# Sinkhorn block attention with a mixture of experts, one core: routing weights spread by GpSimd from a single row, batch 0's second queries laid side by side and transposed whole

## The chip, the cores and the metric

The kernel runs on one core of a Trainium2 chip. The metric is the device time of one launch in microseconds (us). A core has TensorE (PE in the profile, its weight loads PEld), VectorE (DVE), ScalarE (ACT), GpSimd (POOL) and SyncE (SP), which run side by side, each in the order of its own instructions, and wait for one another on semaphores. TensorE writes into PSUM; VectorE and ScalarE carry results from there to SBUF. DMAs are issued by an engine's queue (here SP's and POOL's) and carried out by 16 shared DMA engines.

## The reference

Two parts, the second on the output of the first. Shapes: 4 batches, 8 heads, 768 tokens, head size 64; 8 blocks of 96 tokens; 4 experts with 512 inputs, 1024 hidden units, 512 outputs.

```python
for _ in range(5):                       # P = sort_net, [4, 8, 8, 8]
    P = np.exp(P - P.max(-1, keepdims=True))
    P = P / (P.sum(-1, keepdims=True) + 1e-9)
    P = P / (P.sum(-2, keepdims=True) + 1e-9)
k_sorted = einsum('bhij,bhjcd->bhicd', P, k_blocks)     # v likewise
scores = q_blocks @ k_sorted.T / sqrt(64)               # within each block
attn = softmax(scores) @ v_sorted
x = attn.transpose(0, 2, 1, 3).reshape(3072, 512)
p = domain_probs / (domain_probs.sum(-1, keepdims=True) + 1e-9)
out = sum(p[:, e:e+1] * (np.maximum(x @ w1[e], 0) @ w2[e]) for e in range(4))
```

## The kernel before

**Batch 0 first, then chunks.** The Sinkhorn rounds (L310 to L330, ScalarE's exponentials and VectorE's sums on 32 partitions) stand at the start. Meanwhile TensorE runs matmuls on a constant tile (`warm`, L276) and transposes the first half of batch 0's queries. Batch 0's attention is written out by hand (from L1390 on) in quarters, so that expert 0's first layer (`group0`, L704) can begin before the attention is done. From then on the experts work in 12 chunks of 256 tokens, `(b, c)` with three chunks a batch: `chunk_first` (L815) computes a group of hidden units into one of two PSUM tiles (`psM`, two buffers), and VectorE's L821 applies the ReLU and the routing weight and writes the tile `Hb`; the second layer (L799, L860, in the last chunks L1296) uses a scheme of block sums made by VectorE (L770 to L791). Attention stages of the following batch are put between these by a plan of slots (`PLANS`): `st_q` transposes queries by DMA (L413), `st_v` and `st_k` mix the values and keys (L391, L425), `st_s` and `st_a` compute scores and outputs (L444, L479). In the last chunks POOL multiplies by the routing weight (L1166).

**The routing weights.** L821 multiplies hidden units (on partitions) by a weight that depends on the token (along the row), so every partition needs the same row of weights. VectorE normalises `domain_probs` (`spread_weights`, L246 to L252) and SP writes the result to a scratch tensor `p_dram` in DRAM, in two parts (L256, the first batch; L258, the rest). `load_p` (L230) then reads `p_dram` back with a broadcast over 128 partitions, into a tile `pb` of 4 experts x 256 tokens in f32, of which there is one buffer. Chunk (0, 0) loads all four experts' rows; expert 1's row of chunk (0, 1) is loaded by `load_p_one` (L241) into the place of the first queries (`Tt[3]`), and experts 2 and 3 of that chunk by L230 within `chunk(0, 0)`. Expert 0 of batch 0 doesn't use `pb`.

**Batch 0's queries.** They are loaded into `q0` (in `Tt[3]`) in two halves (L152), with heads of group 0 on partitions 0 to 63 and of group 1 on 64 to 127. `h_q` (L288) transposes 64x64 pieces, 24 a group, into PSUM and a copy brings them to `qT0`. The first half goes by `h_q` with ScalarE's copies (L292), the second by `h_q_both` (two groups, one PSUM tile, then a copy on VectorE and one on ScalarE, L301) as the first of the steps in `later`, which `next_stages` puts between the matmuls of expert 0's second layer (`second_layer0`, L741).

**POOL's queue.** All loads of k, v, q and the weights are POOL's (`load_natural` L113, `load_queries` L126, `load_w1` L139, `load_w2` L146, L1456 and L1475 for parts). There are eight semaphores for them, so that each waits for the landing of the one eight before it. Between them stand POOL's own steps, in the order of the program: masks at the start, `builds(1)` (four multiplies, L364 and L372, which prepare batch 1's mixing matrices), and in `chunk(0, 0)` additions to the output (L953 to L995). `homes`, `sums0` and `sums2` steer where hidden units lie and when weight sums are made; the change doesn't touch them.

**The order around the change.** On ScalarE, batch 0's stretch from 20 us on reads: `h_x(1, act, [0])` (a copy of attention outputs, L628), two evacuations of `group0` (L717), `h_k(0, 1, act)` (mixed keys, L532), two more evacuations, the query copy L301. On POOL: the load of w2 of expert 1, of w2 of expert 2, of w1 of expert 3, of half of w2 of expert 3, `builds(1)`, then batch 1's first loads.

Of the kernel before, what the change touches and what calls it, by code (L numbers as in the profile page):

```python
# [2 lines left out]

# [15 lines left out]
def kernel(  # L19
# [20 lines left out]
    P = 128  # L40
# [182 lines left out]

    pbs = {}

    def load_p(b, c, es=range(E), pb=None):
        if pb is None:
            pb = moe.tile([P, E, 2 * P], F32, name=f"pb_{b}_{c}", tag="pb", bufs=1)
        n = len(es)
        nc.sync.dma_start(  # L230
            pb[:, ds(es[0], n)],
            p_dram[ds(es[0], n), ds(b * S + 2 * c * P, 2 * P)].rearrange("(o e) x -> o e x", o=1).broadcast_to(
                [P, n, 2 * P]
            ),
        )
        return pb

    def load_p_one(b, c, e):

        pb = Tt[3].rearrange("p a f x -> p (a f x)")[:, 0:4 * P].bitcast(F32)  # L240
        nc.sync.dma_start(pb, p_dram[ds(e, 1), ds(b * S + 2 * c * P, 2 * P)].broadcast_to([P, 2 * P]))  # L241
        return pb

    def spread_weights():

        nc.vector.tensor_reduce(p_den, p_in, AX.X, ALU.add)  # L246
        yield
        nc.vector.tensor_scalar(out=p_den, in0=p_den, scalar1=1e-9, scalar2=None, op0=ALU.add)
        yield
        nc.vector.reciprocal(p_den, p_den)  # L250
        yield
        nc.vector.tensor_tensor(  # L252
            p_out.rearrange("p e t -> p t e"), p_in, p_den.broadcast_to([P, NT, E]), ALU.mult
        )
        p_rows = p_dram.rearrange("e (p t) -> p e t", t=NT)
        nc.sync.dma_start(p_rows[0:S_P], p_out[0:S_P])  # L256
        pbs[(0, 0)] = load_p(0, 0)
        nc.sync.dma_start(p_rows[S_P:P], p_out[S_P:P])  # L258
        yield

# [11 lines left out]
    def warm(n):  # L272
        ps = psM.tile([P, 4, P], F32, tag="ps", name=f"ps_w_{state['n']}")
        state["n"] += 1
        for m in range(n):
            nc.tensor.matmul(ps[:, m % 4, :], dummy, dummy, start=True, stop=True)  # L276
# [3 lines left out]
    def h_q(qd, hf, copy, ps=None):  # L280

        if ps is None:
            ps = psa([P, 2, R, 64], F16, f"ps_q_{qd}_{hf}")
        rows = ds(64 * qd, 64)
        for sg in range(2):
            for r in range(R):
                for hh in range(2):
                    nc.tensor.transpose(  # L288
                        ps[ds(D * hh, D), sg, r, :], q0[rows, hf, 2 * sg + hh, r, :], ident[rows, rows]
                    )  # L290
        if copy:
            copy(qT0[qd][:, :, hf], ps[:])  # L292

    def h_q_both(hf, copy):

        ps = psa([P, 2, 1024], F16, f"ps_q_{hf}")
        pss = [ps[:, qd, 0:2 * R * 64].rearrange("p (s r x) -> p s r x", s=2, r=R) for qd in range(2)]
        for qd in range(2):
            h_q(qd, hf, None, pss[qd])
        for qd in range(2):  # L300
            copy[qd](qT0[qd][:, :, hf], pss[qd])  # L301


    srow = const.tile([GH, NB, 1], F32, name="srow")
    scol = const.tile([GH, NB, 1], F32, name="scol")
    sn16 = const.tile([GH, NB, NB, CP], F16, name="sn16")
    warm(84)
    p_steps = spread_weights()
    for it in range(5):
        nc.scalar.activation(sn[:], sn[:], AF.Exp, bias=0.0, scale=1.0)  # L310
# [226 lines left out]
    def h_k(qd, hf, copy, pool=psa):  # L537
        mixed("k", qd, mix_half("k", qd, hf, pool), 0, HB, copy)
# [295 lines left out]
    def chunk(b, c, slot, done=()):  # L834
# [120 lines left out]
        def f2():  # L955
            tt(oa1, product("p2", blk(1, 0), "b21"), oa1, ALU.add)
            slot()
# [522 lines left out]
    builds(1)  # L1480

    later = [
        [(h_q_both, 1, (vec, act)), (h_w, 1, vec)],
        [(h_s, 0, 2), (h_s, 1, 2)],
        [(h_w, 0, vec)],
        [(h_a, 0, 2)],
# [10 lines left out]
                f(*args)  # L1497

    second_layer0(0, next_stages)
    load_queries(1, range(2))  # L1500
    load_natural(1, "v", 0, 2, lambda: load_w2_part(3, DH))
    load_natural(1, "k", 0, 2)
    load_natural(1, "v", 1)
    load_natural(1, "k", 1)
    chunk_first(0, 0, [1, 2], 1, next_stages)
    pb_1 = load_p_one(0, 1, 1)
    h_sums(1, 4)
    for w in range(1, 5):
        h_sums(2, w)
# [41 lines left out]
_INS = ['q', 'k', 'v', 'sort_net', 'moe_domain_probs', 'moe_w1', 'moe_w2']  # L1551
_OUTS = [((3072, 512), 'float32')]
# [25 lines left out]
```

## Time and profile before

| What | Before |
|---|---|
| median of 3 runs | 358.61 us (358.37 to 359.99) |
| the profiled execution | 358.21 us |
| its span | 356.3 us |
| DMA traffic | 40.26 MB, mean 113 GB/s |
| HBM | 41.88 MB read, 6.34 MB written |
| `pb<-p_dram` of 512 KB (4 of them) | 5.8 us from issue to landing, median |
| `pb<-p_dram` of 384 KB (3) | 7.1 us |
| `T<-p_dram` of 128 KB (1) | 12.6 us |
| w loads of 1024 KB (4) | 27.2 us |

The span is the time from the first to the last record of the profiled execution; the rest of its 358.21 us lies around it. Busy times of engines overlap. An instruction's row gives its start, its length, its engine and line, the tile written and the ones read, with their shape; in brackets stands how long its engine had been idle before it and what ended that. A DMA's time from issue to landing holds its waiting behind other transfers.

### The profile page before, as it was taken

Reading aid. Unit: us, or ns where it says so; the run is one execution under the profiler, and the core shown is the slowest. Engines: PE = TensorE matmul, PEld = TensorE weight load, DVE = VectorE, ACT = ScalarE, POOL = GpSimd, SP = SyncE. Lnnn points to the kernel's source line nnn. Section 1 sums busy time; section 2 is a strip of 40 time slices with the busy share of each in tenths; the row PEclk is TensorE's granted clock in tenths of the full one; section 3 lists DMA queues with packets and bytes.
Section 4 is the critical chain, followed back from the end, with each engine's and each line's share of the span. In section 5 each row is a group of like instructions: output and inputs, shape, how many; then the busy total and the mean of one; then the engine's idle time right before and its main releaser. Section 6 shows DMA issues by size and latency. Waiting matters only on the chain.

```text
span 356.3 us, 9511 instructions
## 1 busy us (share of the span) xinstructions
PE 350.4 (98%) x3948; PEld 305.5 (86%) x3948; DVE 277.5 (78%) x555; ACT 170.1 (48%) x302; POOL 137.6 (39%) x154
## 2 busy tenths in 40 slices
PE   8899999999999999999999999999999999999996
PEld 8686857888888888988899888888888888888886
DVE  5766787779798687778879988896678886588963
ACT  2653330452425445368847259830288611598301
POOL 8766112466022420000626318840068800188400
PEclk9999999999999999999999999999999999999999
DMA  8999999999999999743995410005200014100021
GB/s 104 203 205 230 212 209 194 207 195 167 195 180 166 195 116 203 138 88 44 180 205 91 107 74 0 2 1 136 78 26 3 2 37 141 62 0 2 0 75 46
DMA packets 74762, 40.26 MB, mean 113 GB/s; under 512 B 41568, under 2 KB 70496, under 8 KB 74720
## 3 DMA queue, kind: packets, MB, share of 16 engines
q0 software_dynamic: 38720, 19.93, 43.2%
q1 hardware_dynamic: 35856, 19.67, 27.2%
q8 instruction: 31, 0.51, 0.6%
q14 instruction: 11, 0.09, 0.1%
q10 hardware_dynamic: 144, 0.07, 0.1%
HBM read 41.88 MB, written 6.34 MB: 135 GB/s over the span
## 4 chain that ended last, share of the span: by engine, by line
PE 95%; DVE 3%; issue 0%; DMA 0%; ACT 0%; DVEq 0%
PE ps_h L815 18%; PE ps_Q L1296 18%; PE ps_p L799 12%; PE ps_X L1153 10%; PE ps_Z L1153 7%; PE ps_Q L1153 7%; PE ps_Z L1296 6%; PE ps_h L704 3%; PE ps_o L741 3%; PE ps_p L860 3%; PE ps_a L479 2%; PE ps_s L444 2%; PE ps_k L425 1%; PE ps_v L391 1%; PE ps_mv L521 1%; PE ps_a L593 0%
## 5 line engine op out<-in xcount | busy, mean ns | idle before, releaser
L815 PE MATMUL ps_h<-xT,w 128*128 128x256 f16 x576 | 67.5, 273 | 0.0
L815 PEld LDWEIGHTS <-w 128*128 128x128 f16 x576 | 55.2, 98 | 7.3
L821 DVE SCALAR_TENSOR_TENSOR Hb<-ps_h,pb 128x1024 f16<-128x1024 f32 x34 | 41.5, 1223 | 17.8 <-PE ps_h L815 17.6
L1153 PEld LDWEIGHTS <-w 128*128 128x128 f16 x480 | 43.6, 98 | 4.7
L1166 POOL TENSOR_TENSOR arena<-tmp,pb 128x512 f16<-128x512 f32 x12 | 15.2, 1276 | 65.7 <-PE ps_Z L1153 49.8
L1296 PEld LDWEIGHTS <-Hb 128*128 128x128 f16 x320 | 31.1, 98 | 3.5
L1165 ACT ACTIVATE tmp<-tmp 128x512 f32<-128x512 f32 x46 | 29.0, 632 | 3.9 <-DVE tmp L1203 3.9
L1296 PEld LDWEIGHTS <-Sb 128*128 128x128 f16 x304 | 28.2, 98 | 3.0
L1153 PEld LDWEIGHTS <-arena 128*128 128x128 f16 x312 | 27.7, 98 | 2.8
L451 ACT ACTIVATE ET<-ps_s 96x768 f16<-96x768 f32 x24 | 18.1, 802 | 25.2 <-PE ps_s L444 25.0
L434 ACT CAST kT<-ps_k 64x384 f16<-64x384 f32 x48 | 22.7, 473 | 13.3 <-PE ps_k L425 12.3
L126 POOL DMA_DIRECT2D arena<-in_q_dram x24 | 19.9, 842 | 20.8 <-DMA q_ring<-arena 17.7
L1153 PE MATMUL ps_X<-ET,arena 128*128 128x256 f16 x168 | 25.2, 272 | 0.0
L1296 PE MATMUL ps_Q<-w,Hb 128*128 128x256 f16 x192 | 24.6, 273 | 0.0
L799 PEld LDWEIGHTS <-Hb 128*128 128x128 f16 x232 | 21.9, 98 | 3.0
L1159 DVE SCALAR_TENSOR_TENSOR Hb<-ps_X,pb 128x512 f16<-128x512 f32 x27 | 18.7, 692 | 7.0 <-PE ps_X L1153 7.0
L1173 ACT COPY ps_X<-ps_Z 128x512 f32<-128x512 f32 x27 | 15.4, 571 | 17.8 <-PE ps_Z L1153 17.8
L1153 PE MATMUL ps_Z<-xT,w 128*128 128x256 f16 (+1 forms) x176 | 22.5, 258 | 0.0
L785 DVE TENSOR_TENSOR Sb<-Hb 128x512 f16<-128x512 f16 x33 | 20.6, 646 | 0.0
L1180 ACT COPY tmp<-ps_X 128x512 f32<-128x512 f32 x26 | 15.2, 586 | 9.2 <-PE ps_X L1153 6.6
L1159 DVE SCALAR_TENSOR_TENSOR Hb<-ps_Z,pb 128x512 f16<-128x512 f32 x27 | 18.4, 683 | 1.3 <-PE ps_Z L1153 1.3
L1203 DVE TENSOR_TENSOR tmp<-ps_Q,tmp 128x512 f32<-128x512 f32 x26 | 17.7, 683 | 0.8 <-PE ps_Q L1153 0.8
(270 smaller groups left out, 744.3 us busy)
## 6 DMA issues: line engine op xcount, KB each, us to landing
w<-in_moe_w_dram POOLq DMA_DIRECT2D x4, 1024.0 KB, 27.2
w<-in_moe_w_dram POOLq DMA_DIRECT2D x6, 512.0 KB, 19.7
arena<-in_k_dram POOLq DMA_DIRECT2D x7, 384.0 KB, 7.6
arena<-in_v_dram POOLq DMA_DIRECT2D x7, 384.0 KB, 8.1
vs<-arena SPq DMA_DIRECT2D x36, 66.0 KB, 5.3
arena<-in_q_dram POOLq DMA_DIRECT2D x24, 96.0 KB, 7.5
out_dram<-ob SPq DMA_DIRECT2D x9, 256.0 KB, 2.0
pb<-p_dram SPq DMA_DIRECT2D x4, 512.0 KB, 5.8
```

The source lines that it names most:

```text
L126: nc.gpsimd.dma_start(t[:, h // 2, :, h % 2, :], q[b, h].rearrange("(t p) d -> p t d", p=P))
L434: nc.scalar.copy(kT[ds(D * hh, D), r], pk[ds(D * r, D), hh].rearrange("p a (i c) -> p a i c", c=CP),)
L451: nc.scalar.activation(ETs[2 * (pr % 2) + hh][:, 0:S].rearrange("c (a x) -> c a x", a=2), pss[hh][0:BLK, :, 0:HS], AF.Exp, bias=0.0, scale ...
L785: tt(sm[0], blk(0, 1), blk(1, 1), ALU.add)
L799: nc.tensor.matmul(ps, lhs(e, f), Ts[e][rhs][:, f, :], start=(first and e == es[0] and f == 0), stop=(done and e == es[-1] and f == KH - 1 ...
L815: nc.tensor.matmul(ps[:, f, :], w1sb[e][:, kc, ds((4 * g + f) * P, P)], xT[:, kc, ds(2 * c * P, 2 * P)], start=(kc == 0), stop=(kc == NKC ...
L821: nc.vector.scalar_tensor_tensor(out=Hb[:, homes.get(e, e), ds(4 * g, 4), :], in0=ps[:], scalar=0.0, op0=ALU.max, in1=weights(e).broadcast ...
L1153: nc.tensor.matmul(dst[:, ds(f * cols, cols)], a[lhs][:, k, ds((f0 + f) * P, P)], t[rhs][:, k, :], start=(first and f == 0 and k == 0), st ...
L1159: nc.vector.scalar_tensor_tensor(out=home(i, j), in0=src.rearrange("p (f x) -> p f x", f=m), scalar=0.0, op0=ALU.max, in1=weight(j).broadc ...
L1165: nc.scalar.activation(src, src, AF.Relu, bias=0.0, scale=1.0)
L1203: tt(t12, Q, u2, ALU.add)
L1296: nc.tensor.matmul(ps, lhs(e, f), Ts[e][rhs][:, f, part], start=(first and e == 0 and f == 0), stop=(e == E - 1 and f == KH - 1), skip_gro ...
```

## The change

- `load_p_one` and chunk (0, 0)'s and (0, 1)'s share of `load_p` are replaced: SP reads the rows of `p_dram` into partition 0 of the tile alone (`load_rows`), and POOL copies partition 0 to all 128 (`spread`, an instruction `partition_broadcast` from a GpSimd library that is loaded for it, after the load of w2 of expert 1). Chunk (0, 0) reads experts 1 to 3 only. The first `spread` stands between the loads of w2 of experts 1 and 2, the one for (0, 1)'s expert 1 ahead of batch 1's first query loads, the last in `chunk(0, 0)`. POOL's multiplies after the load run from the new library, which has them too; the library that was there first is loaded again at the end. Chunks from (0, 2) on are as before.
- The second half of batch 0's queries: ScalarE copies it from `q0` into `q1` (in `Tt[1]`), with two groups' heads beside each other in a row of 128 (`pair_q`, 128x1536 f16), and `half_q` transposes 12 pieces of 128x128 instead of 48 of 64x64. The two copies out of PSUM stay, with another stride.
- `h_x(1, ..., [0])` copies on VectorE instead of ScalarE.
- The first warm-up block has 69 matmuls instead of 84.

```diff
+    def pb_tile(b, c):
+        return moe.tile([P, E, 2 * P], F32, name=f"pb_{b}_{c}", tag="pb", bufs=1)
...
     def load_p_one(b, c, e):
         pb = Tt[3].rearrange("p a f x -> p (a f x)")[:, 0:4 * P].bitcast(F32)
-        nc.sync.dma_start(pb, p_dram[ds(e, 1), ds(b * S + 2 * c * P, 2 * P)].broadcast_to([P, 2 * P]))
+        pb = pb.rearrange("p (o x) -> p o x", o=1)
+        load_rows(pb, b, c, [e])
+        spread(pb)
         return pb
+
+    def load_rows(dst, b, c, es):
+        nc.sync.dma_start(
+            dst[0:1], p_dram[ds(es[0], len(es)), ds(b * S + 2 * c * P, 2 * P)].rearrange("(o e) x -> o e x", o=1)
+        )
+
+    def spread(dst):
+        nc.gpsimd.partition_broadcast(dst, dst[0:1])
...
-        pbs[(0, 0)] = load_p(0, 0)
+        pbs[(0, 0)] = pb_tile(0, 0)
+        load_rows(pbs[(0, 0)][:, 1:E], 0, 0, range(1, E))
...
+    q1 = Tt[1].rearrange("p a f x -> p (a f x)")[:, 0:2 * R * P].rearrange("p (s r x) -> p s r x", s=2, r=R)
+
+    def pair_q():
+        nc.scalar.copy(
+            q1.rearrange("p s r (h d) -> p s h r d", h=2),
+            q0[:, 1].rearrange("p (s h) r d -> p s h r d", h=2),
+        )
+
+    def half_q(copies):
+        ps = psa([P, 2, 1024], F16, "ps_q1")
+        for sg in range(2):
+            for r in range(R):
+                nc.tensor.transpose(ps[:, sg, ds(r * P, P)], q1[:, sg, r], ident[:])
         for qd in range(2):
-            h_q(qd, hf, None, pss[qd])
-        for qd in range(2):
-            copy[qd](qT0[qd][:, :, hf], pss[qd])
+            copies[qd](
+                qT0[qd][:, :, 1],
+                ps[:, :, 0:R * P].rearrange("p s (r q x) -> p s r q x", r=R, q=2)[:, :, :, qd],
+            )
...
-    warm(84)
+    warm(69)
...
-        pbs[nxt] = load_p(*nxt, range(first, first + 1))
-        rest = lambda: load_p(*nxt, range(first + 1, E), pbs[nxt])
         late = b == c == 1
-        if not late:
-            rest()
+        if nxt == (0, 1):
+            pbs[nxt] = pb_tile(*nxt)
+            load_rows(pbs[nxt][:, 2:E], *nxt, range(2, E))
+        else:
+            pbs[nxt] = load_p(*nxt, range(first, first + 1))
+            rest = lambda: load_p(*nxt, range(first + 1, E), pbs[nxt])
+            if not late:
+                rest()
...
         f2()
+        spread(pbs[nxt][:, 2:E])
         next(steps)
...
-    h_x(1, act, [0], ps_s01)
+    h_x(1, vec, [0], ps_s01)
     evacuate00()
...
     h_k(0, 1, act)
+    pair_q()
     group0(1, 1, 0, [0, 1])
...
     load_w2(1)
+    nc.gpsimd.load_library(library_config.all_libraries[10])
+    spread(pbs[(0, 0)][:, 1:E])
     load_w2(2)
...
-        [(h_q_both, 1, (vec, act)), (h_w, 1, vec)],
+        [(half_q, (vec, act)), (h_w, 1, vec)],
...
     second_layer0(0, next_stages)
+    pb_1 = load_p_one(0, 1, 1)
     load_queries(1, range(2))
...
     chunk_first(0, 0, [1, 2], 1, next_stages)
-    pb_1 = load_p_one(0, 1, 1)
...
-    chunk_first(0, 1, [1], 1, next_stages, lambda e: pb_1.rearrange("p (o x) -> p o x", o=1))
+    chunk_first(0, 1, [1], 1, next_stages, lambda e: pb_1)
...
         last_second(g + 1, upper=True)
+    nc.gpsimd.load_library(library_config.standard)
```

More of the change, by code (lines that the diff above doesn't have):

```diff
@@ L5 @@
 import concourse.tile as tile
-from concourse import mybir
+from concourse import library_config, mybir
 from concourse.bass import ds
@@ L224 @@
     pbs = {}
+    def pb_tile(b, c):
+        return moe.tile([P, E, 2 * P], F32, name=f"pb_{b}_{c}", tag="pb", bufs=1)
     def load_p(b, c, es=range(E), pb=None):
         if pb is None:
-            pb = moe.tile([P, E, 2 * P], F32, name=f"pb_{b}_{c}", tag="pb", bufs=1)
+            pb = pb_tile(b, c)
         n = len(es)
@@ L292, in h_q @@
             copy(qT0[qd][:, :, hf], ps[:])
-    def h_q_both(hf, copy):
-        ps = psa([P, 2, 1024], F16, f"ps_q_{hf}")
-        pss = [ps[:, qd, 0:2 * R * 64].rearrange("p (s r x) -> p s r x", s=2, r=R) for qd in range(2)]
+    q1 = Tt[1].rearrange("p a f x -> p (a f x)")[:, 0:2 * R * P].rearrange("p (s r x) -> p s r x", s=2, r=R)
[9 more added lines that the diff above has]
+                nc.tensor.transpose(ps[:, sg, ds(r * P, P)], q1[:, sg, r], ident[:])
         for qd in range(2):
-            h_q(qd, hf, None, pss[qd])
-        for qd in range(2):
-            copy[qd](qT0[qd][:, :, hf], pss[qd])
+            copies[qd](
+                qT0[qd][:, :, 1],
+                ps[:, :, 0:R * P].rearrange("p s (r q x) -> p s r q x", r=R, q=2)[:, :, :, qd],
+            )
     srow = const.tile([GH, NB, 1], F32, name="srow")
```

## The prediction

> **What bounds the kernel now.** I read the page's busy shares first, then the chain of waits, then the timeline of the stretches the change touches (the start to 12 us, 18 to 48 us, 62 to 76 us), and last the DMA issues there. The busy shares and the chain:
>
> ```profile
> PE 350.4 (98%) x3948; PEld 305.5 (86%) x3948; DVE 277.5 (78%) x555; ACT 170.1 (48%) x302; POOL 137.6 (39%) x154
> ...
> PE 95%; DVE 3%; issue 0%; DMA 0%; ACT 0%; DVEq 0%
> ```
>
> The chain that ended last is TensorE work for 95% of 356.3 us. The 3% of VectorE is nearly all before 11.60 us, in the five Sinkhorn rounds; no DMA stands in it. So TensorE work taken out of the chain is worth its length, a DMA or POOL step brought forward is worth nothing, and one made late costs as soon as TensorE runs out of other work.
>
> **The fewer warm-up matmuls** (84 to 69). Timeline of the start (start, length, engine, line; idle before in brackets):
>
> ```profile
> 1.06 6.74 PE L276 MATMUL ps_w<-Hb 128*128 128x128 f16 x84 [1.06 <-DVE Hb L157]
> ...
> 8.51 1.85 PE L276 MATMUL ps_w<-Hb 128*128 128x128 f16 x30
> 11.60 0.26 PE L342 MATMUL ps_R<-ident,sn 32*128 32x32 f16 x4 [1.24 <-DVE sn L330]
> ```
>
> Late warm-up matmuls take 1.85/30 = 62 ns, so 15 fewer end TensorE's lead-in 15 x 62 = 0.9 us sooner. The next step, L342, waits for VectorE's L330 whatever TensorE does, so the 0.9 us turns into idle time: 1.24 becomes about 2.1 us. The first query transposes between the two blocks need DMAs issued at 1.28 and 2.0 us that took 4.1 and 4.2 us: there by 6.2, before the 6.9 us at which they would now start. Cost 0; if the idle time slows what follows, rival D.
>
> **Forty-eight small transposes become twelve full ones.** From the chain of waits, first the ones removed, then the nearest full-width ones:
>
> ```profile
> 28.79 0.78 PE ps_q L288 x45
> 29.57 0.58 PE ps_w L548 x8
> ```
>
> L288 takes 0.78 us of the chain. Twelve full ones cost 12 x 62 = 0.74 us by the warm-up row, 12 x 0.58/8 = 0.87 us by L548's: between -0.04 and +0.09 us. I take 0: fewer instructions, not less time. The two copies out of PSUM (L301: VectorE 0.56, ScalarE 0.80 us) keep their 128x768 elements and their order: 0.
>
> **The ScalarE copy that lays the queries side by side** (`pair_q`) is new, 128x1536 f16, queued behind L532's second key copy:
>
> ```profile
> 23.81 0.82 ACT L532 CAST kT<-ps_mk 128x768 f16<-128x768 f32 x1
> 26.32 0.81 ACT L717 ACTIVATE Hb<-ps_h 128x768 f16<-128x768 f32 x1 [1.69 <-PE ps_h L704]
> ```
>
> L532 takes 0.48 us for 384 elements and 0.82 for 768, so 0.34 per 384 more and 0.82 + 2 x 0.34 = 1.50 us for 1536 (two copies of 768 as L292's would be 1.6). It runs 24.63 to 26.13 or 26.23, within the 1.69 us of idle time. Behind it waits L717, whose PSUM tile L741 at 27.76 needs; L717 ended at 27.13, so there are 0.6 us more. Moving `h_x(1, ..., [0])` from ScalarE (0.48 at 22.05) to VectorE (0.56 by its twin at 24.39) starts ScalarE up to 0.4 us sooner; VectorE had nothing from 21.93 to 23.02. Its input, the second query halves, was issued at 12.40 and 13.0 us and took 10.0 and 10.2: there at 23.2, before 24.2. Cost 0; without that cover, each us of `pair_q` beyond 0.8 us of slack is a us on TensorE.
>
> **The weights of the experts: rows and a POOL broadcast for a broadcasting DMA.** Removed before 40 us: one DMA of 512 KB (three quarters of it needed) and one of 128 KB, and later 384 KB; each is now a DMA of 1 to 3 KB into one partition, and a `partition_broadcast` on POOL. A library load comes ahead of the first, and POOL runs in order, so everything behind it slides: three weight loads, four builds, then the loads of batch 1. POOL before (its timeline), then the reader of the tile and what VectorE does behind it (VectorE's timeline):
>
> ```profile
> 21.71 1.76 POOL L146 DMA_DIRECT2D w<-in_moe_w_dram  x2 [0.38 <-DMA w<-in_moe_w_dram]
> 23.50 0.75 POOL L139 DMA_DIRECT2D w<-in_moe_w_dram  x1
> 26.10 0.89 POOL L1475 DMA_DIRECT2D w<-in_moe_w_dram  x1 [1.86 <-DMA w<-in_moe_w_dram]
> ```
>
> ```profile
> 38.79 1.23 DVE L821 SCALAR_TENSOR_TENSOR Hb<-ps_h,pb 128x1024 f16<-128x1024 f32 x1 [1.63 <-PE ps_h L815]
> 39.93 0.19 DVE L606 RECIPROCAL rz<-ps_a 96x8 f32<-96x8 f32 x1
> 40.15 0.69 DVE L607 TENSOR_TENSOR xsl<-ps_a,rz 96x512 f16<-96x512 f32 x1
> 40.78 1.23 DVE L821 SCALAR_TENSOR_TENSOR Hb<-ps_h,pb 128x1024 f16<-128x1024 f32 x1
> 41.92 0.19 DVE L606 RECIPROCAL rz<-ps_a 96x8 f32<-96x8 f32 x1
> 42.15 0.69 DVE L607 TENSOR_TENSOR xsl<-ps_a,rz 96x512 f16<-96x512 f32 x1
> ```
>
> The deadline is 38.79: from there VectorE runs without a gap until 42.84, and TensorE's L624 starts at 42.91 on its result. Load and broadcast together may take 38.79 - 22.55 (the load of w2 of expert 1 is out by then) = 16.2 us; each us beyond is one on TensorE.
>
> *The load.* No row shows one. From below: the only table load in the trace, ScalarE's at 0.74 us, 1.28 us. From above: a load whose code comes through busy DMA engines as late as the slowest transfer issued in this stretch, 33.3 us (L1475's). Nearest are the small transfers on the other queue at the same time: 5.5 us (12 KB), 12.2 (36 KB), 12.6 (128 KB). I take 10 us.
>
> [...]
>
> *The broadcast.* Also without a row: POOL's 128x128 copy took 0.30 us (L194 0.29), so 768 elements are 0.30 if size hardly counts and 6 x 0.30 = 1.8 us in proportion; from above, the DMA that did the same, 10.4 us. I take 1.8. Its rows are asked for at 25.51, once the p_dram write of 5.5 us is in, and are there by 31.0 (5.5, as the 12 KB took) or 35.9 at worst (10.4). So the broadcast ends at 32.6 + 1.8 = 34.4, or 37.7 with the latest rows: 4.4 or 1.1 us ahead of the deadline. Cost 0, with ends of 0 and (22.55 + 33.3 + 10.4 - 38.79) = +27 us.
>
> *What slides behind it.* From 34.4 the three weight loads are issued (0.8 each), the builds run (4 x 1.05), then a broadcast of 256 (0.6): 41.7, and batch 1's first query load goes out there instead of at 31.02. The transfers are behind a queue that stays full: issued at 21.71, w2 of expert 1 took 25.1 us and landed at 46.8; the next two megabytes, issued at 22.6 and 23.5, landed at 51.9 and 56.8, each after what stood ahead of it. So nothing is lost if the next is issued before about 43, and POOL, whose L113 at 47.35 waited for that same landing at 46.8, has caught up there. Against it: 640 KB fewer to move at 1 MB per 4.9 us (51.9 to 56.8) brings later landings 3 us forward, but who waited for them is one TensorE row, L391 at 65.38, with 0.19 us. Gain 0 to 0.2.
>
> *The second chunk's weights.* L230's pair, issued at 63.82, took 8.6 and 7.0 us; L821 reads them at 75.10. Rows in 5.5 us and a broadcast of 512 (1.2 by the same proportion) make 70.5. Behind that broadcast POOL's two query loads go out at 70.5 and 71.3 instead of 65.25 and 66.1. They took 10.8 and 10.7 us, because k's 384 KB, issued at 60.76 with 13.7 us, had to land first, at 74.5; out at 71.3 they are still in time for that place, or, where the queue is 3 us further, land 4.8 us after issue (the shortest of L126): 76.1, against 76.8. L413 transposes them from 76.82 on in 8.3 us, for scores at 86.08: 1.0 us more in hand. POOL's L970 slides from 70.01 to 72.2; it feeds the stores of 72.81 and no TensorE row. Cost 0; if rows or broadcast take 2 us longer, up to 1 us. The second load, of the library that was there first, stands behind POOL's last multiply (329.85 + 3.92 = 333.8 us), with 22 us left: 0.
>
> **Sum.** Against the profiled execution, 358.21 us for a span of 356.3: 0 + 0 + 0 - 0.1 (half of 0 to 0.2) = 358.1. That execution lies 0.4 below the median of the runs shown (358.61), so in their terms 358.4 to 358.5; I forecast 358.4. Less than 0.5% (1.8 us) is about what can't be told from no change here.
>
> **Rivals.**
> A. The forecast, no change: 358.4, its own range 357.4 to 359.8. Chance 0.66.
> B. Slower: the broadcast comes too late, L821 waits and TensorE with it. It decides from 16.2 us of load and broadcast. At 20 + 1.8 us: 22.55 + 21.8 = 44.4, 5.6 us late, 364; with the upper end 385. For it: the DMA engines are at their fullest there, and the weight loads issued from 21.71 on took 25 to 33 us. Against it: small transfers on the other queue took 5.5 to 12.6. Chance 0.17.
> C. Slower: POOL's multiply (L1166, 1.27 us in the last three pairs of chunks) is slower with the other library. Two of them and 0.52 us idle fill 3.06 us, so it decides from 1.53; at 1.8 us, 16 multiplies x 0.27 x 3 stretches = 13 us, 371. Nothing in the trace speaks for another speed. Chance 0.05.
> D. Slower: with 2.1 us idle ahead of L342 TensorE drops to the rate it started at, about double the time a matmul (10 to 13 rows a us up to 5 us, 20 and more after). That would double some 2.6 us of chain pieces between 11.6 and 15.5: 361 at most. Chance 0.03.
> E. Faster: the 1 MB of DMA traffic saved removes small waits that the trace books as "issue". TensorE is idle for 5.9 us in all, 2.3 of them ahead of 11.6; half of the remaining 3.6 is 1.8 us: 356.6. Against it: DMA 0% in the chain. Chance 0.09.
>
> [...]
>
> **Range and chances.** Faster is E, 0.09; same is A, 0.66, with the small end of B: 0.67 in all; slower is the rest of B, C and D, 0.24. From 357.0 to 363.0 leaves out most of E (0.06), the upper half of B (0.08) and C (0.05).
>
> **What would show it.** Right: L821's first row near 38.8 with TensorE as its releaser; the gap of POOL ahead of the broadcast below 15 us; twelve transposes in 0.7 to 0.9 us; L342 at 11.6; weights landing some 3 us earlier with nothing behind them any earlier; L1166 at 1.27. Wrong: L821 released by POOL, or the chain passing through POOL or ScalarE between 24 and 45 us; POOL multiplies above 1.5 us; a span shorter by over 1 us with an unchanged TensorE sum.

## The result, and the profile after

| What | Before | After |
|---|---|---|
| median, 22 executions of each side by side | 358.37 us (357.86 to 359.99) | 359.89 us (357.81 to 365.24) |
| ratio | 1 | 1.0042, 95% interval 1.0026 to 1.0058 |
| the profiled execution | 358.21 us | 361.78 us |
| its span | 356.3 us | 359.8 us |
| its mean granted TensorE clock | 1.000 | 0.991 |

The change is 0.4% slower. The fastest execution is as fast as the fastest before; what is new is the spread. The ratios here and below leave out executions more than 1.5% above the fastest of their kernel (three of the change's 22). The page of the profiled execution after: busy shares, the granted clock in 40 slices of the span, and the chain that ended last.

```profile
PE 352.5 (98%) x3897; PEld 307.6 (85%) x3897; DVE 278.4 (77%) x556; ACT 171.3 (48%) x302; POOL 140.0 (39%) x157
...
PEclk9789999999999999999999999999999999999999
...
PE 89%; DMA 5%; DVE 4%; ACT 1%; issue 0%; ACTq 0%; DVEq 0%
```

TensorE has 51 matmuls fewer (15 warm-ups and 36 transposes) and is busy 2.1 us longer. The second and third slices (9 to 27 us) have a lower clock, and 5% of the chain is now DMA, which had none. What TensorE waited for in this execution (total, times, longest):

```profile
PE ps_R L367 <- DVE sn L355: 1.5, 1, 1.5
PE ps_h L840 <- DVE Hb L846: 1.2, 1, 1.2
PE ps_w L290 <- DVE Hb L157: 1.1, 1, 1.1
PE ps_Q L1183 <- DMA w<-arena: 0.6, 1, 0.6
```

The first and third are the idle times of the start, which were there before. The other two are new, at 98 and 196 us, well after the edited work (the third broadcast is over at 69.3 us). (L840 and L846 are L815 and L821 of before, L1183 is L1153.) Set against the run before instruction by instruction, the 3.5 us of this execution arise mostly at four places: 0.3 us by 11.87 us (a VectorE step of the Sinkhorn rounds took 0.2 us longer), 1.7 us between 13.7 and 21 us, 1.2 us at 98 us, 0.7 us at 196 us; some 0.5 us came back between 22 and 40 us.

**The start.** TensorE's first rows, then windows of the granted clock. In a row of windows the columns are the stretch, its length, five engines' busy times with their counts, the granted clock, the DMA engines' share, GB/s.

```profile
1.05 6.79 PE L290 MATMUL ps_w<-Hb 128*128 128x128 f16 x69 [1.05 <-DVE Hb L157]
...
8.55 1.85 PE L290 MATMUL ps_w<-Hb 128*128 128x128 f16 x30
11.87 0.26 PE L367 MATMUL ps_R<-ident,sn 32*128 32x32 f16 x4 [1.47 <-DVE sn L355]
```

```profile
10.00:13.00 3.00, 1.50 (x39) 1.22 (x37) 2.39 (x8) 1.25 (x2) 2.86 (x14) 1.00 1.30 199
13.00:14.00 1.00, 1.00 (x52) 0.86 (x47) 0.30 (x1) 0.58 (x2) 0.96 (x2) 0.85 1.31 203
14.00:17.00 3.00, 3.00 (x56) 2.51 (x52) 1.76 (x5) 2.25 (x4) 1.24 (x2) 0.50 1.26 205
17.00:20.00 3.00, 3.00 (x56) 2.58 (x51) 1.57 (x4) 2.05 (x3) 2.82 (x4) 0.50 1.25 205
20.00:21.00 1.00, 1.00 (x20) 1.00 (x18) 0.22 (x2) 0.48 (x1) 0.64 (x1) 0.73 1.29 200
```

The 69 warm-ups took as long as the 84 did (6.79 against 6.74 us), because the first rise of the clock came later in this execution (6.88 us against 5.04): a warm-up takes 107 ns before it and 56 ns after. After the idle time of 1.47 us the clock is halved for 6.8 us, from 13.7 to 20.5.

**GpSimd.** The weights for the first chunk, and the reader on VectorE:

```profile
21.79 0.88 POOL L146 DMA_DIRECT2D w<-in_moe_w_dram  x1 [0.31 <-DMA w<-in_moe_w_dram]
32.48 1.05 POOL L255 PARTITION_BROADCAST pb<-pb  x1 [9.81 <-DMA pb<-p_dram]
33.38 1.07 POOL L146 DMA_DIRECT2D w<-in_moe_w_dram  x1
```

```profile
40.32 1.23 DVE L846 SCALAR_TENSOR_TENSOR Hb<-ps_h,pb 128x1024 f16<-128x1024 f32 x1 [1.70 <-POOL arena L389]
```

The broadcast of 768 elements took 1.05 us and was done at 33.5, so the reader at 40.32 had 6.8 us in hand. (The bracket names a POOL step that happened to end at 40.20; L846's own matmuls end at 38.30 + 1.92 = 40.22, and its idle time is the same 1.70 us in kernels where the bracket names something else.)

### The profile page after: what moved, and what is told of

Its sections match the earlier page's. It is cut to its first block, busy times and chain, and to the rows that moved or that the text cites. A ratio compares the mean times of both kernels' runs of the same rounds, so it can differ in the third digit from the quotient of the medians.

```text
span 359.8 us, 9418 instructions
## 1 busy us (share of the span) xinstructions
PE 352.5 (98%) x3897; PEld 307.6 (85%) x3897; DVE 278.4 (77%) x556; ACT 171.3 (48%) x302; POOL 140.0 (39%) x157
## 4 chain that ended last, share of the span: by engine, by line
PE 89%; DMA 5%; DVE 4%; ACT 1%; issue 0%; ACTq 0%; DVEq 0%
PE ps_Q L1326 17%; PE ps_h L840 17%; PE ps_p L824 10%; PE ps_X L1183 9%; PE ps_Z L1326 6%; PE ps_Q L1183 6%; PE ps_Z L1183 6%; PE ps_o L766 3%; PE ps_h L729 3%; PE ps_p L889 3%; DMA pb<-p_dram 2%; DMA w<-arena 2%; PE ps_a L504 1%; PE ps_s L469 1%; PE ps_v L416 1%; PE ps_k L450 1%
## 5 line engine op out<-in xcount | busy, mean ns | idle before, releaser
L840 PE MATMUL ps_h<-xT,w 128*128 128x256 f16 x576 | 67.5, 273 | 1.2 <-DVE Hb L846 1.2
L840 PEld LDWEIGHTS <-w 128*128 128x128 f16 x576 | 55.3, 98 | 8.5 <-issue 1.3
L846 DVE SCALAR_TENSOR_TENSOR Hb<-ps_h,pb 128x1024 f16<-128x1024 f32 x34 | 41.4, 1223 | 19.3 <-PE ps_h L840 14.7
L1183 PEld LDWEIGHTS <-w 128*128 128x128 f16 x480 | 43.6, 98 | 5.6 <-DMA w<-arena 0.9
L1196 POOL TENSOR_TENSOR arena<-tmp,pb 128x512 f16<-128x512 f32 x12 | 15.2, 1275 | 65.8 <-PE ps_Z L1183 49.8
L1183 PEld LDWEIGHTS <-arena 128*128 128x128 f16 x312 | 27.7, 98 | 2.8
L1183 PE MATMUL ps_X<-ET,arena 128*128 128x256 f16 x168 | 25.2, 272 | 0.0
L1183 PE MATMUL ps_Z<-xT,w 128*128 128x256 f16 (+1 forms) x176 | 22.5, 258 | 0.0
L810 DVE TENSOR_TENSOR Sb<-Hb 128x512 f16<-128x512 f16 x33 | 20.5, 644 | 0.0
```

What stands on the lines that cost most here:

```text
L810: tt(sm[0], blk(0, 1), blk(1, 1), ALU.add)
L840: nc.tensor.matmul(ps[:, f, :], w1sb[e][:, kc, ds((4 * g + f) * P, P)], xT[:, kc, ds(2 * c * P, 2 * P)], start=(kc == 0), stop=(kc == NKC ...
L846: nc.vector.scalar_tensor_tensor(out=Hb[:, homes.get(e, e), ds(4 * g, 4), :], in0=ps[:], scalar=0.0, op0=ALU.max, in1=weights(e).broadcast ...
L1183: nc.tensor.matmul(dst[:, ds(f * cols, cols)], a[lhs][:, k, ds((f0 + f) * P, P)], t[rhs][:, k, :], start=(first and f == 0 and k == 0), st ...
```

## Experiments

The first four runs took the obvious parts apart.

**84 warm-ups again** (the changed kernel otherwise).

```diff
-    warm(69)
+    warm(84)
```

> The changed kernel with 84 warm-up matmuls instead of 69, nothing else. Theory 1 (the shorter warm-up leaves TensorE idle for 1.5 to 2 us ahead of L342's successor, the granted clock falls to 0.5 for some 6.5 us after 13.9 us, and that is most of the loss): clock 1.0, the matmuls between 14 and 20 us back to their length of before, 358.0 to 358.7, same as before. Rival 2 (the broadcasts on POOL and what they push back on SP's queue are the loss, the stall at 98 us): still 359.3 or more. Rival 3 (the side-by-side queries): still 359.3 or more.

Measured: 359.27 us (357.89 to 363.75), ratio 1.0029 [1.0003, 1.0055], 10 of 12 executions at a clock of 0.999 or 1.0. The clock of the start is mended, and by the medians more than half of the loss stays (0.9 of 1.5 us). That is close to the 359.3 or more of the rivals.

**69 warm-ups alone** (the kernel before otherwise).

```diff
-    warm(84)
+    warm(69)
```

> The kernel before with 69 warm-up matmuls instead of 84, nothing else. Theory 1: slower than before by 0.7 to 3 us (359.1 to 361.4), the clock below 1.0 in most executions. Rivals 2 and 3: 358.4, as before, clock 1.0.

Measured: 359.02 us (358.64 to 361.09), ratio 1.0019 [1.0003, 1.0035], 8 of 12 executions with a mean clock of 0.986 to 0.995. Fewer warm-ups are not free.

**The changed kernel with 50 matmuls in the second warm-up block instead of 30**, to fill the idle time.

```diff
-            warm(30)
+            warm(50)
```

> The changed kernel with its 69 warm-ups, and the second block of warm-ups (after the first query transposes) 50 long instead of 30, so that TensorE is busy until about 11.5 us. Theory 1, that it is the idle time ahead of the first real matmul: clock 1.0, 358.0 to 358.7. If the clock hangs on the number ahead of the transposes instead (how soon it first rises), it still falls: 359.3 or more. Rivals 2 and 3: 359.3 or more.

Measured: 363.46 us (361.18 to 364.14), ratio 1.0129 [1.0102, 1.0155]. The expected 358.0 to 358.7 us was missed by some 5 us. The profiled execution kept its clock in the start and lost elsewhere: TensorE waited 0.6 us for `vs<-arena` at 124 us and 2.1 us for `w<-arena`, and behind that wait the clock fell too:

```profile
PE ps_Q L1183 <- DMA w<-arena: 2.1, 1, 2.1
...
PE ps_a L504 <- DMA vs<-arena: 0.6, 1, 0.6
```

```profile
186.00:195.00 9.00, 7.25 (x120) 6.73 (x117) 6.33 (x10) 5.30 (x10) 5.31 (x5) 1.00 1.21 160
195.00:200.00 5.00, 4.67 (x43) 3.97 (x44) 2.08 (x3) 1.95 (x4) 3.18 (x3) 0.66 0.26 40
```

The offset against an undisturbed run grows by 2.2 us at the wait and to 4.3 us four microseconds later.

**With 84 warm-ups, experts 2 and 3 of chunk (0, 1) by a broadcasting DMA again.**

```diff
-            pbs[nxt] = pb_tile(*nxt)
-            load_rows(pbs[nxt][:, 2:E], *nxt, range(2, E))
+            pbs[nxt] = load_p(*nxt, range(2, E))
...
-        spread(pbs[nxt][:, 2:E])
```

> The changed kernel with 84 warm-ups, and chunk (0, 1)'s experts 2 and 3 loaded by the broadcasting DMA again (no third broadcast on POOL). Theory 1 alone: the same as with 84 warm-ups only, to 0.2 us. If the third broadcast also costs through SP's queue (the weights of chunk (0, 2) late at 98 us): 0.3 to 1.2 us faster than with 84 warm-ups only.

Measured: 361.09 us (358.44 to 364.99), ratio 1.0041 [1.0016, 1.0066]: no better. So the third broadcast, which I suspected for the wait at 98 us, isn't the rest of the loss by itself, although its profiled execution (358.44 us, one of the fastest) has no wait at that place.

The next three cut the change along its parts, each put alone into the kernel before, with 84 warm-ups.

**The queries' part alone** (`pair_q`, `half_q`, `h_x(1, vec, [0])`, as in the diff of the change).

> The kernel before with the queries' part of the change alone: pair_q on ScalarE, half_q's twelve full transposes, h_x(1, ..., [0]) on VectorE; 84 warm-ups and the broadcasting DMAs as before. Theory (the loss that is left with 84 warm-ups comes from the shifted DMAs and POOL's queue): as before, 358.1 to 358.7 us, ratio 0.999 to 1.001. Rival (the side-by-side queries cost it): some 359.2 us, ratio 1.002 to 1.004, with a stall of TensorE between 24 and 36 us or a later first L840 row.

Measured: 359.95 us (358.87 to 363.5), ratio 1.0058 [1.0031, 1.0084]. The rival, not the theory: the part costed at nothing is slower by itself, by no less than all of the rest.

**The routing weights' part alone** (rows, broadcasts, both library loads).

> The kernel before with the routing weights' part alone: library load, rows into one partition, three broadcasts on POOL, the load at the end; 84 warm-ups and the old transposes of queries. Theory: it keeps all that the run with 84 warm-ups lost, 359.0 to 359.5 us, ratio 1.002 to 1.004, with executions up to 2 us above its fastest, and stalls behind late DMAs near 95 to 100 or 190 to 197 us. Rival (queries): as before, 358.1 to 358.7 us.

Measured: 358.46 us (358.05 to 359.67), ratio 1.0005 [0.9993, 1.0017]. The theory of the shifted DMAs fell here: this part has no cost that can be told from none.

**The two library loads alone.**

```diff
     load_w2(1)
+    nc.gpsimd.load_library(library_config.all_libraries[10])
     load_w2(2)
...
+    nc.gpsimd.load_library(library_config.standard)
```

> The kernel before with the two library loads alone (at the places that they have in the change); the weights still come by the broadcasting DMAs, and POOL's multiplies run from the new library. It tells the load from the broadcasts. If the load and its hold on POOL's queue of weight loads are the cost: 359.0 to 359.5 us. If the cost is in the broadcasts and in the DMAs that come earlier for the removed 640 KB: 358.2 to 358.7 us, as before.

Measured: 358.43 us (357.96 to 359.92), ratio 1.0006 [0.9994, 1.0017]. Free.

Of the queries' part, TensorE's twelve transposes were no slower in the trace (0.67 us of the chain where 48 took 0.78). But the trace holds one more kind of record. While the kernel runs, queue q8, which the page calls "instruction", has 31 packets of 16 KB spread over the span, from 11.1 to 350.4 us. That they are TensorE's code is inferred: TensorE has some 7,900 instructions, matmuls and weight loads, which makes 255 for each of 31 packets. The runs below take a block to be 256, and test it.

```profile
q8 instruction: 31, 0.51, 0.6%
q14 instruction: 11, 0.09, 0.1%
```

(The page of before: queue, packets, MB, share.) Taking 36 matmuls and their weight loads out is 72 instructions, so by this reading every later block begins 72 instructions further on in the work. The new theory: that shift is what costs. Three runs split it from the rest.

**ScalarE's and VectorE's share of the queries' part alone.** The copy is made and read by nothing; the 48 transposes stay.

```diff
+    pair_q()
...
-    h_x(1, act, [0], ps_s01)
+    h_x(1, vec, [0], ps_s01)
```

> The kernel before with ScalarE's copy that lays the queries side by side and h_x(1, ..., [0]) on VectorE, but with the 48 old transposes, which read the first place (the copy's result is read by nothing). TensorE's program is as before to the instruction. New theory (what costs is that TensorE's program is 72 instructions shorter from 29 us on, so that the 16 KB blocks in which its code is fetched begin elsewhere in the work): as before, 358.1 to 358.7 us, ratio 0.999 to 1.002. Rival (the copy's time on ScalarE or h_x on VectorE): 359.3 us or more, ratio 1.003 to 1.008, as in the run with the queries' part alone.

Measured: 358.29 us (358.04 to 359.45), ratio 0.9993 [0.9979, 1.0007].

**TensorE's share alone**: twelve full transposes straight from `q0`.

```diff
-        [(h_q_both, 1, (vec, act)), (h_w, 1, vec)],
+        [(half_q, (vec, act)), (h_w, 1, vec)],
...
-                nc.tensor.transpose(ps[:, sg, ds(r * P, P)], q1[:, sg, r], ident[:])
+                nc.tensor.transpose(ps[:, sg, ds(r * P, P)], q2[:, sg * R + r], ident[:])
```

> The kernel before with twelve full transposes in the place of the 48, read straight from q0 in pairs of rows of one head: it leaves out the laying side by side, so batch 0's second queries are in wrong order. ScalarE and VectorE work as before; TensorE's program is 72 instructions shorter. New theory (place of the code blocks): 359.3 to 360.3 us, ratio 1.003 to 1.008, with some executions 2 to 5 us above the fastest and some with 3 us instead of 2 around the span. Rival (the copy, h_x): as before, 358.1 to 358.7 us.

Measured: 359.18 us (358.01 to 363.31), ratio 1.0026 [0.9998, 1.0054]. The spread is there, with 4 of 12 executions under 358.4 and two over 362.5; but the interval reaches 1, so this run alone doesn't show a loss.

**The queries' part with the program's length restored** by 72 weight loads that nothing uses.

```diff
     nc.tensor.matmul(
         ps, h0(fc)[:, ds(t * P, P)], w2sb[0][:, fc, :],
         start=(fc == 0), stop=(fc == NFC - 1),
     )
+    if hf == 0:
+        for _ in range(3):
+            nc.tensor.ldweights(ident[0:32, 0:32])
```

> The queries' part alone, with 72 weight loads of 32x32 that nothing uses put between the 24 matmuls of 512 columns of expert 0's second layer right around the transposes, so that TensorE's program is as long as before again and its code blocks from 36 us on begin where they did. New theory: back to 358.1 to 358.8 us, ratio 0.999 to 1.002 (0.2 us more if the weight loads are not hidden). Rival (the copy, h_x or the full transposes themselves): stays at 359.5 us or more, ratio 1.003 to 1.008.

Measured: 357.93 us (357.66 to 358.37), ratio 0.9983 [0.9971, 0.9995]. 2 us less than the same kernel without these loads (1.0058 [1.0031, 1.0084]), the spread is gone, and it is the fastest kernel of this study, faster than before and after. Why it is faster than before isn't shown. Four of the matmuls beside the loads still take 1.03 us, so the loads are hidden.

The last four close the account.

**The kernel before with nothing but a shift of the blocks**: 184 unused weight loads, since 184 and -72 are the same place in a block of 256.

```diff
+    for _ in range(4 * (hf == 0 or t < 2 or fc < 6)):
+        nc.tensor.ldweights(ident[0:32, 0:32])
```

> The kernel before with nothing changed but 184 weight loads of 32x32 that nothing uses, four beside each of 46 matmuls of 512 columns of expert 0's second layer (28 to 52 us); 256 less 72 is 184, so from there on the 16 KB code blocks begin at the same instructions as after the change's 72 fewer, with all of the work unchanged. Theory (place of the code blocks): slower as with the twelve transposes alone, 358.8 to 360.3 us, ratio 1.002 to 1.006, some executions at 361 and over, the w<-arena of 184 us landing at 192 or later instead of 190. Rival (the shorter program costs in another way, or the unused weight loads of the other run helped by themselves): as before or faster, 357.9 to 358.6 us.

Measured: 359.78 us (358.68 to 361.63), ratio 1.0032 [1.0008, 1.0055]. Unchanged work with moved blocks is slower. The packets of q8 agree with the 256: with 184 more they lie within 0.7 us of those with 72 fewer (start of four of them, us):

```
before                  62.27   73.76   86.41   98.15
queries + 72 loads      62.05   74.26   87.02   97.69
queries' part           65.13   75.36   92.30  100.94
184 loads               65.54   75.75   92.91  100.82
```

Its waits of TensorE, and a piece of its chain near 31 us (start, length, what):

```profile
PE ps_Q L1155 <- DMA w<-arena: 1.6, 1, 1.6
...
PE ps_o L741 <- issue: 0.4, 1, 0.4
```

```profile
30.37 0.43 PE ps_o L741 x2
30.80 0.40 issue
31.20 0.61 PE ps_o L741 x2
```

The two make 2.0 of the 2.2 us by which its span (358.5) is longer than before's. The 0.40 us stand between two matmuls of one group, and the trace names nothing that ended them. They end 2.4 us after the start of a packet of q8 (28.80), so I read them as missing code. That one may be a cost of the added loads as much as of the shift: they begin in this stretch. A run with 256 such loads, behind which the blocks would stand as before, wasn't made, so the loads' own cost isn't wholly set apart; but the wait of 1.6 us comes some 140 us after the last of them.

**The whole change with 84 warm-ups and 72 such loads.**

```diff
-    warm(69)
+    warm(84)
...
+    for _ in range(3 * (hf == 0)):
+        nc.tensor.ldweights(ident[0:32, 0:32])
```

> The changed kernel with 84 warm-ups and 72 unused weight loads beside the 24 matmuls of the first half of expert 0's second layer: code blocks as before, all else of the change kept (library, rows and broadcasts, queries side by side). Theory (the two losses are the clock after the shorter warm-up and the place of the code blocks, and the rest of the change is worth what the queries' part with such loads is): 357.7 to 358.4 us, ratio 0.998 to 1.000, within 1 us of each other. Rival (the broadcasts have a cost of their own together with the queries): 358.8 us or more.

Measured: 358.35 us (357.88 to 362.72), ratio 1.0014 [0.9989, 1.0039]. The median is what was expected, 1.5 us under the change's, but the interval overlaps those of the change and of the run with 84 warm-ups; ten of twelve executions lie between 357.88 and 359.13, but two stand at 361.92 and 362.72 with a clock of 0.995, which the theory did not expect.

**The change as it is with 102 such loads** (72 and twice the 15 warm-ups).

```diff
+    for _ in range((4 + (t == 0 and fc < 6)) * (hf == 0)):
+        nc.tensor.ldweights(ident[0:32, 0:32])
```

> The changed kernel as it is (69 warm-ups) with 102 unused weight loads beside the same 24 matmuls: code blocks as before from 36 us on. Theory: the loss by the clock in the start stays (358.3 to 359.5 us, most executions with a mean clock of 0.985 to 0.995, the fastest at 357.7), that by the code blocks goes. Rival (the shorter warm-up costs by the place of the code blocks too): 357.7 to 358.3 us with nearly all executions at a clock of 1.0.

Measured: 359.6 us (358.05 to 363.46), ratio 1.0034 [1.0019, 1.0048], 10 of 12 executions below a clock of 1. As expected, though somewhat slower: the clock's part of the loss stays.

**69 warm-ups alone with 30 such loads.**

```diff
-    warm(84)
+    warm(69)
...
+    for _ in range((1 + (t == 0 and fc < 6)) * (hf == 0)):
+        nc.tensor.ldweights(ident[0:32, 0:32])
```

> The kernel before with 69 warm-ups and 30 unused weight loads beside the same 24 matmuls: code blocks as before from 36 us on. Theory (clock): as the run with 69 warm-ups alone, 358.7 to 359.4 us, ratio 1.001 to 1.003, with most executions below a mean clock of 1.0. Rival (code blocks): as before, 358.0 to 358.5 us.

Measured: 359.06 us (357.88 to 360.63), ratio 1.0017 [1.0003, 1.0031], as without the loads. The warm-ups' loss is the clock's, not the blocks'. By mean clock its executions fall into steps of some 0.005, which at half the clock is some 3.6 us of the span (2 x 0.005 x 357 us), about half of the 6.83 us in the profiled execution of the change, and each step is worth 0.7 to 1.0 us between medians:

```
mean clock   executions of this kernel (us)
1.000        357.88  358.04  359.01
0.995        358.70  358.71  358.77  359.11  359.36
0.990        359.72  359.80  360.02
0.986        360.63
```

## Why the prediction was wrong

The forecast was no change, 358.4 us; it came to 359.9. Two steps failed, and both had been costed at nothing. Each is shown by itself in the kernel before; a third, smaller one was seen in the trace.

**The fewer warm-ups: "Cost 0; if the idle time slows what follows, rival D."** The idle time did slow what follows. Rival D had 0.03, and it was right in kind: with 84 warm-ups again 10 of 12 executions kept their clock; with 69 alone, 8 of 12 didn't. D put the doubling between 11.6 and 15.5 us and bounded it at 361; the clock in fact stayed up until 13.7 and was half until 20.5, and the chain there lost 1.7 us in the profiled execution. What the trace of before could have told: its clock was never tested by an idle time beyond 1.24 us, and that it would bear 2.1 as well was shown by no run. In the change's profiled execution the clock rose at 6.88, fell at 13.71 and rose at 20.54 us, 6.83 us apart each time; the idle time there was 1.47 us, from 10.40 to 11.87.

The length of the idle time doesn't decide by itself, and the moment of the first rise differs from execution to execution. From the start of five profiled executions (rise of the clock, idle time ahead of the Sinkhorn's transposes, then the clock):

```
kernel                    rise   idle           clock after it
after                     6.88   10.40-11.87    half from 13.71 for 6.83 us
after, 102 loads          6.14   10.04-11.68    half from 12.96 for 6.83 us
69 warm-ups alone         4.13    9.09-12.05    stays 1.00
before                    5.04   10.36-11.60    stays 1.00
queries' part             5.45   10.56-12.07    stays 1.00
```

The longest idle time, 2.96 us, kept its clock, and so did 1.51 us with the queries' part, while 1.47 and 1.68 us lost it. The two that lost it have the latest rises of the five, 6.88 and 6.14 us against 5.45 at most. A late rise doesn't do it alone: with 84 warm-ups in the changed kernel, 49 of them from 4.76 us on took 3.94 us where they took 3.04 before, which by 107 and 56 ns a warm-up puts its rise at some 6.9 us (an estimate); there the idle time was 0.40 us, and the clock stayed 1.00. So of these six executions the two that lost it are the ones with both, a late rise and an idle time of over a us; what ties the fall to the rise isn't shown, nor is which idle time is too long. Shown is that 84 instead of 69 keeps the clock in 10 of 12 executions, against 5 of 22 (with 84 and the broadcasting DMA in 6 of 12; where the other six lost it isn't shown).

**The transposes: "I take 0: fewer instructions, not less time."** Their own time was right (0.67 us of the chain against a price of 0.74 by the warm-up row, 0.78 before). What I left out is that fewer instructions are a change in themselves. With 72 instructions less the later packets of q8, read here as fetches of TensorE's code, come at another moment of the work (65.13 us where it was 62.27). The runs that show this: the same work 72 shorter is slower with the copy (and by the median without it, 359.18), the copy alone is not, and restoring the length takes the loss away (359.95 to 357.93 us), while moving the blocks under unchanged work makes it (359.78). One place where it costs can be read in the DMA chain before `w<-arena`, which in the kernel before lands 2.8 us ahead of the matmul that needs it (190.0, 192.8). POOL's issues and the landings that the trace records, in profiled executions (a fetch is a packet of q8, by its start):

```
kernel                  2nd arena<-w   fetch at  4th arena<-w   w<-arena lands  TensorE waits
                        issue + us               issue + us                     for it
before                  170.1 + 6.66   173.8     174.4 + 6.94   190.0           -
copy alone              169.9 + 6.82   173.7     174.3 + 7.75   192.8           -
weights' part alone     170.1 + 6.34   173.7     174.5 + 8.96   191.6           -
queries + 72 loads      169.7 + 6.40   173.2     174.1 + 7.50   190.1           -
transposes alone        170.2 + 5.73   175.8     174.6 + 8.44   192.5           -
queries' part           170.6 + 5.83   176.7     175.0 + 8.74   193.6           some 0.3
184 loads               170.5 + 5.86   178.4     174.9 + 9.62   194.9           1.6
after                   172.8 + 5.76   179.2     177.2 + 9.27   196.2           0.6
after, 50 in block two  170.4 + 5.84   175.9     174.7 + 9.48   195.3           2.1
```

Read the second column first: where the fetch falls between issue and landing of that DMA it takes 6.3 to 7.0 us, where the fetch comes at its end or later 5.7 to 5.9, without an exception among sixteen traces. Moved by 2 to 5 us, the fetch falls into the fourth DMA instead, which takes 8.4 to 9.8 us where all but one of the others are below 7.8. That is a coincidence in time and not a test: with 69 warm-ups alone the fetch (175.5) falls into both, and the fourth still took 6.9. The following steps of the chain each wait for the one before, and the last lands 2 to 6 us later (2.7 us of that, in the change, are its start 2.7 us late). TensorE's rows there, first with 184 loads, then with the queries' part and 72 loads:

```profile
192.77 0.60 PE L1298 MATMUL ps_Q<-w,Hb 128*128 128x256 f16 x4
194.97 0.62 PE L1155 MATMUL ps_Q<-xT,w 128*128 128x128 f16 x8 [1.60 <-DMA w<-arena]
```

```profile
192.03 0.60 PE L1310 MATMUL ps_Q<-w,Hb 128*128 128x256 f16 x4
192.46 0.61 PE L1167 MATMUL ps_Q<-xT,w 128*128 128x128 f16 x8
```

The second goes on without a gap, with the tile landed 2.3 us earlier. That chain varies between profiled executions too: the weights' part alone has one long step without a shift, and the copy alone lands at 192.82, just ahead of a matmul at 192.87. That a shifted kernel loses in some executions and not in others, which is the spread seen, would follow from this.

It isn't the only place. Of the 2.0 us that the profiled execution of the queries' part lost, 0.3 us lie at `w<-arena` and 1.2 us outside the span. Between 2.4 and 4.1 us instead of 1.9 to 2.1 lie around the span in 3 of 8 executions with the queries' part, 3 of 12 with the transposes alone, 3 of 12 with the change and 84 warm-ups, and 2 of 12 with 184 loads. These are four of the five kernels whose blocks are moved by 72 or 184 instructions; no execution of the fifth or of any other kernel has more than 2.1. The remaining 0.5 us come from its start, where the profile lists two waits without a releaser:

```profile
PE ps_s L559 <- issue: 0.6, 1, 0.6
PE ps_R L353 <- issue: 0.2, 1, 0.2
```

They end at 20.66 and 14.20 us, ahead of the transposes at 29.82, so the shift can't have made them. The prediction had stopped at engines and at the DMAs that the kernel issues; the packets of q8 are on the same page, two lines further down.

**The second chunk's weights: "it feeds the stores of 72.81 and no TensorE row. Cost 0".** Half wrong. The broadcast came at 68.52 us and POOL's two query loads behind it at 69.16, both a little earlier than the 70.5 that I gave. But I did not follow the queue behind them: the next four query loads went out at 75.04 instead of 73.60, SP's second transposing DMA waited for them (82.73 instead of 79.33), and `pb` for chunk (0, 2), last in SP's queue, was asked for at 89.07 instead of 85.22 and landed at 97.93. VectorE was there before:

```profile
98.02 2.36 DVE L846 SCALAR_TENSOR_TENSOR Hb<-ps_h,pb 128x1024 f16<-128x1024 f32 x2 [2.73 <-DMA pb<-p_dram]
```

It cost 1.2 us in the profiled execution, 0.5 with 84 warm-ups, 0.3 with the 72 loads as well, and nothing that the view lists with the weights' part alone. The landing was later in all four: 97.93, 95.46, 95.30 and 95.25 us, against 92.89 before. So the broadcast uses up the reserve; what decides whether TensorE then waits isn't shown, since it waited 0.3 us with clock and blocks both mended. "If rows or broadcast take 2 us longer, up to 1 us" was about the right size for the wrong cause, by luck.

**What held.** The library load and the first broadcast (rival B, 0.17): load, rows and broadcast were over 10.9 us after POOL came free at 22.67 (priced 11.9, deadline 16.2). POOL's 9.81 us idle end with the rows' landing, so the load is within that; its own length isn't seen. The broadcasts were cheaper than the proportion I took: 0.55, 0.80 and 1.05 us for 256, 512 and 768 elements (1.8 taken for the last). Rival C: L1196, the former L1166, is at 1.28 us as before. Rival E: no sign. `pair_q` took 1.48 us (1.50 worked out), and the matmuls behind it waited for nothing. Later weights landed 3.1 us earlier (w2 of expert 1 at 43.7, w1 of expert 3 at 53.7), as worked out, and TensorE had not waited for them.

**How the loss divides.** Medians: the change 359.9; with the code blocks restored 359.6; with the clock restored (84 warm-ups) 359.3; with both 358.35; before 358.4. By the medians either mend alone brings 0.3 to 0.6 us and both together all of it. That what is lost at one place is in part hidden behind a wait at the other would explain this, but it is argued; the intervals of these runs overlap, so how the loss divides inside the change isn't shown. Open are the two executions near 362 us with both mended: the profile isn't of one of these, and the third broadcast's wait at 98 us (0.3 us in the profiled one) is only a guess.

## What to carry to other kernels

Idle time in the lead-in isn't free only because the next step waits for another engine: here 1.47 us of it, in an execution whose clock first rose at 6.88 us, were followed by 6.83 us at half the clock, and 2.96 us after a rise at 4.13 us were not. So look at the clock of several executions before warm-ups that look useless go (with 69 alone 8 of 12 lost it). Here 72 TensorE instructions fewer moved the later packets of q8 (62.27 to 65.13 us) and cost up to 0.6%, so a kernel whose DMA chains land near their deadline can win or lose some 0.3 to 0.6%, as here, by its length alone; before a small edit is judged, give the program its old length with unused weight loads in the shade of wide matmuls, and compare spreads as well as medians. When POOL or SP gets a new waiting step, follow its queue to the end, through the loads behind it to the transposes on the other queue that wait for those.

## What the runs showed of the hardware

- Queue q8, "instruction" on the page, carried packets of 16 KB: 31 before, with 7,896 instructions of TensorE, and 30 after, with 7,794. They are read as TensorE's code in blocks of 256 instructions: 184 more put a packet at 65.54 us and 72 fewer at 65.13, where it was 62.27 before. In the kernel before one came every 6 us from 11 to 35 us and every 6.5 to 18 us later; a packet took 0.9 to 1.6 us there. The second 256 KB DMA of the chain above took 6.3 to 7.0 us with a packet inside and 5.7 to 5.9 without.
- Four idle times of TensorE that no wait explains ended 2.2 to 2.4 us after the start of a packet of q8, and are read as missing code: at 31.20 for a fetch at 28.80 (184 loads), at 14.20 and 20.66 for fetches at 11.96 and 18.30 (queries' part), at 32.80 for one at 30.46 (69 warm-ups with 30 loads).
- With the queries' part a packet of q8 began at 359.40 us, after a span of 357.1, in an execution with 3.1 us around the span. In 3 of its 8 executions 2.9 to 3.1 us instead of 2.0 lay there; before had 1.9 to 2.1 us in each of 35. That the fetch is the cause is read from this one trace.
- After a single wait of 2.1 us at 193 us (the changed kernel with 50 matmuls in the second block) the clock was down to 0.66 over 195 to 200 us, and the offset grew from 2.2 to 4.3 us.
